# Spreading 23 guard bounds over the rows by a store to DRAM and a broadcast load

## The chip, the cores and the metric

The kernel runs on one core of a Trainium2 chip. The metric is device time in microseconds for one execution, measured over three runs; a profiled execution beside them gives the trace. The engines are called as in the profile: PE (TensorE matmul), PEld (its weight loads), DVE (VectorE), ACT (ScalarE), POOL (GpSimd) and SP (SyncE, which here only issues DMAs).

## The reference

Two attention blocks over 2048 rows with 32 heads of 32, whose outputs stand side by side.

```python
# A: plain multi-head attention
qkv = x @ wqkv                       # x 2048x1024, wqkv 1024x3072
scores = q @ k.T * Dh ** -0.5        # per head, 2048x2048
o = softmax(scores) @ v
a = o @ wo
# B: four segments of 512 rows, causal attention in each, and a memory
for s in range(4):
    p = softmax(qs @ ks.T * scale + mask)
    a_dot = p @ vs
    a_mem = phi(qs) @ M / (phi(qs) @ z + 1e-6)
    o = g * a_mem + (1 - g) * a_dot  # g = sigmoid(beta), per head
    M, z = M + phi(ks).T @ vs, z + sum(phi(ks))
b = o @ wo
return concatenate([a, b], axis=-1)
```

Here phi(t) is t + 1 for positive t and exp(t) otherwise.

## The kernel before, in words

**Units of work.** Part A is worked in groups g of four heads (8 groups) and blocks c of 256 queries (8 blocks); part B in segments s and groups j. For each set of tiles PE makes scores in PSUM (line 964, four heads side by side), ACT turns them into P by an exponential (line 1044, up to 128 x 1024 at a time), and PE multiplies P by V and by ones (the PV rounds of lines 1140 and 1147, in one accumulator bank). P lies in a ring of 20 buffers of 512 columns, so that an exponential writes a buffer only when the PV rounds that read its old content are done. 118 tiles take a cubic instead of an exponential, on DVE and POOL (lines 1002 to 1007).

**The shared bank.** Six PSUM banks hold scores and one the PV accumulators. Bank 6 (X_BANKS) is left for everything else: the projections of K, Q and V, the output projections, the memory's products, and the guard blocks. Each job has a turn: PE fills the bank (line 601 for the projections, through `steps`), DVE empties it (line 1315), and the next job follows. `xbank()` opens a turn.

**The guards.** The softmax subtracts no maximum. In its place each block of keys and queries has a bound, minus half the scale times the sum of the largest squared norms of k and of q, and a flag that tells whether any bound is low enough to matter. Every exponential has two forms, plain and with the bound as its bias. At the first exponential of a block ACT waits for the flag, loads it (line 559) and branches; as long as no flag is set it runs the plain form. A guard block has two steps. `guard_cols` squares and sums K and Q (POOL squares, line 1340 on PE, and a DVE maximum at line 1347), and leaves one column of `cols` with a number for each of 128 rows. `guard_end` has to bring the largest of all rows, or of each half of them, to all rows: DVE copies the column 32 wide into `dg` (line 1384, rounded up by UP because dg is bf16), PE multiplies it by `pick` into a further turn of bank 6 (the spread, line 1393, four matmuls for each column), and DVE takes the maximum out of PSUM (line 1401). Three or four tiny DVE steps make the bias (lines 1407 to 1414) and the flag (line 1418).

There are 27 guard blocks. Four stand in the start of part A and are urgent (`guard_more` and the first quarter). The other 23 are the groups 1 to 7 of part A (`guard_A`, two columns each, one for K and one for Q) and the four pairs of groups in each of the four segments of part B (one column each, K in the first 64 rows and Q in the last 64).

**The order.** No engine's program is written by hand. The code plans operations with keys, durations and dependencies; `level` spreads the jobs between release and due times, and `Prog.schedule` simulates the five engines and writes out one fixed order for each. Its constants (lead times such as LEAD_A, the list NUDGE of due times for single jobs, PHI_AT, AHEAD and others) steer that order. Each engine then runs its order strictly, waiting on semaphores. All DMAs but a few at the start and the end are issued by SP, in one order, so that one that waits holds up those behind it.

Of the kernel before, what the change touches and what calls it, by code (L numbers as in the profile page):

```python
# [6 lines left out]
dt = mybir.dt  # L7
ACT = mybir.ActivationFunctionType
ALU = mybir.AluOpType
AX = mybir.AxisListType  # L10

P = 128
# [24 lines left out]
CARRY = 7  # L37
WHOLE = (("A", 7, 7), ("A", 7, 6))
BCK = 9.626
SOON = 0.124  # L40

PAIR = ((6, 0), (6, 1), (6, 2), (7, 0), (7, 1), (7, 2), (7, 3), (6, 3), (7, 4), (6, 4), (7, 5), (6, 5), (6, 6), (7, 6), (6, 7), (7, 7))
# [113 lines left out]
PV_T = 1.269  # L156
PV_HOT = 1.702
NORM_K = 8.667
JOB_AT = 0.555
# [6 lines left out]
BACKLOG = 2.178  # L166
XR = 9.514
XC = 2.153
STEP = 1.785
OUT3 = 72.703  # L170
OT_STEP = 3
NUDGE = {('KB', 3, 1): 8.43, ('VB', 1, 1): 0.75, ('OB', 0, 0): 7.19, ('OA', 1): 11.77, ('OB', 2, 0): 12, ('KB', 1, 0): 7.83, ('OA', 4): -20.99, ('KA', 5): -6.03, ('KB', 3, 2): 0.67, ('OA', 3): -6.14, ('OA', 5): -5.41, ('VB', 0, 0): -25, ('phi', 3, 1): 4.71, ('KB', 3, 3): 2.86, ('KB', 2, 2): -3.03, ('OA', 0): 0.43, ('VB', 2, 0): 8.32, ('phi', 0, 1): -1.72, ('KB', 1, 1): -7.02, ('phi', 1, 1): 2.49, ('phi', 3, 3): -10.68, ('VB', 1, 0): -3.92, ('OB', 0, 1): 5.6, ('VB', 2, 1): 5.84, ('OB', 3, 0): -0.92, ('VB', 3, 1): -7.84, ('OB', 1, 1): -3.29, ('OB', 1, 0): 1.78, ('KB', 1, 2): -2.71, ('phi', 0, 0): -0.27, ('VB', 0, 1): 9.83, ('OB', 3, 1): 1.59, ('phi', 2, 2): -0.46, ('KB', 2, 1): 8.53, ('VA', 1): -0.13, ('KA', 2): -0.38, ('KB', 2, 0): -4.12, ('phi', 2, 3): 1.64, ('phi', 3, 0): 0.15, ('phi', 0, 2): 3.99, ('phi', 1, 2): -2.16, ('phi', 2, 1): 0.4, ('OA', 2): 6.02, ('phi', 0, 3): -4.43, ('KB', 1, 3): -0.65, ('phi', 1, 0): 0.24, ('KB', 0, 1): -2.16}
SAFE = 0
WOA_STEP = 3
OUT_D = 66.869
M_AT = 4.042
V0_R = 4.52
V0_D = 11.868
FREED = 0.5
VFREED = 11.963  # L180


class Prog:
# [385 lines left out]
class _Kernel:  # L569
# [7 lines left out]
    def sb(self, name, shape, dtype=dt.bfloat16):  # L577
        return self.es.enter_context(self.nc.sbuf_tensor(name, shape, dtype))
# [92 lines left out]
    def alloc(self):  # L671
        nc = self.nc
        sb = self.sb
# [81 lines left out]
        self.bias = sb("bias", [P, 64], dt.float32)  # L755
        self.r_bias = {}
        self.braw = sb("braw", [P, 2], dt.float32)
        self.r_braw = Res()
# [21 lines left out]
        self.sm_last = [self.sem(f"d_last{i}") for i in range(2)]  # L780
        self.sm_PKt = [self.sem(f"d_PKt{i}") for i in range(2)]
        self.sm_OTe = self.sem("d_OTe")

    def plan(self):
        self.plan_constants()
# [203 lines left out]
    def plan_cube(self, t, bank, T):  # L989


        i, j, k = self.ncube % Y_RING, self.ncube % Z_RING, self.ncube % C_RING
        self.ncube += 1
        Y, Z, rY, rZ = self.Y[i], self.Z[j], self.r_Y[i], self.r_Z[j]
        dst, rP = self.Pc[:, k, :], self.r_Pc[k]
        t["P"] = (self.Pc, k, rP)
        bc = t["bias"]
        last = []

        def f(key):  # L1000
# [9 lines left out]
        return (lambda e: e.activation(dst, Y[:, :], ACT.Exp, bias=self.bias[:, 60 + bc:61 + bc], scale=1.0 / KAPPA),  # L1010
                bc, rY, rP, last, t)

    def plan_exp(self, take, slot, buf, T, lo=0, fix=None):
# [364 lines left out]
    def guard_end(self, key, cols, nper, bias_cols, bank=None, urgent=False):  # L1378
        since = len(self.pg.ops)

        dg, rdg = self.dg, self.r_dg
        n = len(cols)
        for i, (c, r) in enumerate(cols):
            self.dve(lambda e, i=i, c=c: e.tensor_scalar(dg[:, i, :], self.cols[:, c:c + 1].to_broadcast([P, 32]), UP, None, ALU.mult),
                     32, key, [r], [rdg], fixed=0.13)
        b = self.xbank() if bank is None else bank

        def spread(e):

            for i in range(n):  # L1390
                for t in range(4):
                    r = slice(32 * t, 32 * t + 32)
                    ins = e.matmul(self.ps[r, 512 * b + 16 * i:512 * b + 16 * i + 16], dg[:, i, :], self.pick[:, :], start=not i, stop=True,
                                   tile_position=(0, 32 * t), skip_group_check=True)
            return ins
# [5 lines left out]
        self.dve(lambda e: e.tensor_reduce(self.cols[:, ci:ci + m],  # L1401
                                           self.ps[:, 512 * b:512 * b + 16 * n].rearrange("p (m r) -> p m r", m=m), AX.X,
                                           ALU.max), 16 * n, key + 0.3, [self.at(b)], [rr])
        for k, bc in enumerate(bias_cols):
            rb = self.r_bias.setdefault(bc, Res())
            raw = self.braw[:, k:k + 1]
            self.dve(lambda e, k=k, raw=raw: e.tensor_scalar(raw, self.cols[:, ci + 2 * k:ci + 2 * k + 1],
                                                             self.cols[:, ci + 2 * k + 1:ci + 2 * k + 2], -0.5 * SCALE,
                                                             ALU.add, ALU.mult), 1, key + 0.4, [rr], [self.r_braw], fixed=0.2)
            self.last_bias = self.dve(lambda e, bc=bc, raw=raw: e.scalar_tensor_tensor(  # L1410
                out=self.bias[:, bc:bc + 1], in0=raw, scalar=-FREE, in1=raw, op0=ALU.is_lt, op1=ALU.mult), 1, key + 0.4,
                [self.r_braw], [rb], fixed=0.3)
            if bc < 2:
                self.dve(lambda e, bc=bc: e.tensor_scalar(self.bias[:, 60 + bc:61 + bc], self.bias[:, bc:bc + 1], ROOT, None, ALU.add), 1,
                         key + 0.4, [rb], [self.r_biasr[bc]])
            nf = self.nflag
            self.nflag += 1
            o = self.dve(lambda e, nf=nf, raw=raw: e.scalar_tensor_tensor(
                out=self.flags[:, nf + 1:nf + 2], in0=raw, scalar=-FREE, in1=self.flags[:, nf:nf + 1], op0=ALU.is_lt, op1=ALU.max), 1,
                key + 0.4, [self.r_braw, self.r_flags], [self.r_flags], fixed=0.17)  # L1420
            self.flag_of[bc] = (nf, o, self.flags[0:1, nf + 1:nf + 2])
        for o in self.pg.ops[since:]:
            if o.eng == "DVE" and urgent:
                o.urgent = True


    def plan_prologue(self):
        self.r_cols = [Res() for _ in range(64)]
# [371 lines left out]
    def plan_jobs(self):  # L1800
# [44 lines left out]
        for s in range(NSEG):  # L1845
# [125 lines left out]
```

## Time and profile before

| What | Value |
|---|---|
| Time, median of three runs | 1117.63 us (1117.24 to 1118.58) |
| Time of the profiled execution | 1116.0 us |
| Span of the profiled execution | 1114.3 us |
| Busy: ACT, PE, DVE, POOL | 1068.6, 1035.5, 732.8, 676.3 us |
| DMA | 72.00 MB, mean 65 GB/s |
| Mean granted clock of TensorE | 0.998 |

The span runs from the first to the last instruction that the profiler recorded. Busy time is the union of an engine's instructions; matmuls overlap in the pipeline, so PE's share is not its distance to a peak. In the groups of instructions a row gives the line, the engine, the operation, what it writes and reads with the shapes, and the count; then the busy time in us and the mean of one in ns, and last the idle time of the engine just before these instructions and what ended it. A line of waits gives who waited for what: us in total, times, and the longest. A line of DMA issues gives the size and the median us from issue to landing. In the window rows each engine has busy time and count, and the granted clock, the DMA share and GB/s stand last.

### The profile page before, as it was taken

How to read it: one execution, taken by the hardware profiler on the slowest of the kernel's cores; microseconds unless marked ns; L12 is line 12 of the kernel's file. 1: busy time of each engine (PE TensorE's matmuls, PEld its weight loads, DVE VectorE, ACT ScalarE, POOL GpSimd, SP SyncE). 2: the span in 40 equal slices, each digit the busy share in tenths (PEclk: the TensorE clock that was granted, in tenths of full speed). 3: DMA queues.
4: the chain of work that ended last, by engine and by line, in shares of the span. 5: the costliest groups of instructions: out<-in, count | busy, mean ns of one | idle time of the engine just before them, and what ended most of it. 6: DMA issues, size and time to landing. Idle time of an engine off the chain costs nothing.

```text
span 1114.3 us, 55312 instructions
## 1 busy us (share of the span) xinstructions
PE 1035.5 (93%) x25332; PEld 558.1 (50%) x25332; DVE 732.8 (66%) x1567; ACT 1068.6 (96%) x1224; POOL 676.3 (61%) x654
## 2 busy tenths in 40 slices
PE   8999999999999988899899988999899899899998
PEld 4456545555545544456455444556455444444554
DVE  3345667766675587877775787777744867856544
ACT  4989999999999999999999999999999899999997
POOL 2224676856576575866666686775845777747421
PEclk9999999999999999999999999999999999999999
DMA  9032351015213230132322320143030351012201
GB/s 208 10 85 49 79 126 24 15 19 122 63 48 88 65 94 12 24 80 57 93 49 63 97 52 18 24 83 88 17 87 29 103 190 41 20 45 62 79 23 54
DMA packets 171098, 72.00 MB, mean 65 GB/s; under 512 B 134768, under 2 KB 169072, under 8 KB 170864
## 3 DMA queue, kind: packets, MB, share of 16 engines
q1 hardware_dynamic: 168496, 67.66, 24.5%
q8 instruction: 199, 3.26, 1.2%
q10 hardware_dynamic: 2368, 0.79, 0.3%
q14 instruction: 35, 0.29, 0.1%
HBM read 45.23 MB, written 11.67 MB: 51 GB/s over the span
## 4 chain that ended last, share of the span: by engine, by line
ACT 44%; PE 40%; DVE 8%; POOL 4%; issue 2%; SPq 1%; DMA 0%; ACTq 0%; DVEq 0%
ACT P L1044 42%; PE ps L601 19%; PE ps L964 8%; PE ps L1140 6%; PE ps L1147 5%; PE ps L1563 1%; POOL Z L1005 1%; DVE Pc L1007 1%; ACT PKQ_B L1607 1%; DVE PKQ_B L1612 1%; SPq L1284 1%; DVE rc L1172 1%; POOL Z L1006 1%; DVE Y L1002 1%; POOL P L1064 1%
## 5 line engine op out<-in xcount | busy, mean ns | idle before, releaser
L1044 ACT ACTIVATE P<-ps 128x1024 bf16<-128x1024 f32 (+1 forms) x1176 | 1041.9, 1084 | 25.7 <-PE ps L1147 19.5
L1147 PE MATMUL ps<-P,onesb 128*32 128x256 bf16 (+1 forms) x4628 | 296.6, 270 | 0.0
L1005 POOL TENSOR_SCALAR Z<-Y 128x512 f32<-128x512 f32 x118 | 181.5, 1538 | 167.2 <-DVE Y L1002 164.5
L1140 PE MATMUL ps<-P,V_A 128*32 128x256 bf16 x3860 | 254.0, 274 | 5.4 <-DVE T L1168 2.3
L964 PE MATMUL ps<-KQ_A 32*128 32x256 bf16 x4096 | 203.4, 273 | 27.8 <-ACT P L1044 20.4
L1006 POOL TENSOR_TENSOR Z<-Z,Y 128x512 f32<-128x512 f32 x118 | 152.4, 1292 | 4.8
L1147 PEld LDWEIGHTS ps<-P,onesb 128*32 128x32 bf16 x4628 | 129.4, 97 | 36.2 <-issue 13.3
L964 PEld LDWEIGHTS ps<-KQ_A 32*128 32x128 bf16 x4096 | 61.4, 92 | 169.9 <-ACT P L1044 139.2
L601 PE MATMUL ps<-xT_B,W_B 128*32 128x512 bf16 (+1 forms) x2232 | 139.3, 366 | 2.1 <-DVE cols L1347 1.2
L601 PE MATMUL ps<-xT_A,W_A 128*32 128x512 bf16 (+1 forms) x2236 | 136.4, 363 | 3.8 <-DVE KQ_A L1315 1.2
L1002 DVE TENSOR_SCALAR Y<-ps 128x512 f32<-128x512 f32 x118 | 81.4, 690 | 79.8 <-PE ps L964 78.5
L1140 PEld LDWEIGHTS ps<-P,V_A 128*32 128x32 bf16 x3860 | 108.6, 96 | 42.5 <-issue 14.2
L1064 POOL TENSOR_SCALAR_AFFINE_SELECT P<-P 128x768 bf16<-128x768 bf16 (+1 forms) x96 | 76.2, 797 | 78.7 <-ACT P L1044 77.6
L1329 POOL TENSOR_TENSOR sqA<-KQ_A 128x512 bf16<-128x512 bf16 x61 | 65.6, 1079 | 93.5 <-DVE KQ_A L1315 64.8
L1007 DVE SCALAR_TENSOR_TENSOR Pc<-Z,Y 128x512 bf16<-128x512 f32 x118 | 105.2, 892 | 21.4 <-POOL Z L1006 14.8
L1329 POOL TENSOR_TENSOR sqB<-KQ_B 128x512 bf16<-128x512 bf16 x64 | 71.1, 1114 | 44.9 <-DVE KQ_B L1315 33.1
L1165 DVE STREAM_TRANSPOSE T<-ps 128x256 f32<-128x256 f32 (+1 forms) x148 | 71.9, 487 | 21.3 <-PE ps L1147 12.9
L601 PEld LDWEIGHTS ps<-xT_A,W_A 128*32 128x32 bf16 x2236 | 52.0, 96 | 53.2 <-issue 15.8
L601 PEld LDWEIGHTS ps<-xT_B,W_B 128*32 128x32 bf16 x2232 | 51.0, 96 | 51.1 <-issue 20.6
L1180 DVE STREAM_TRANSPOSE T<-rc 128x256 f32<-128x256 f32 (+1 forms) x152 | 72.0, 478 | 2.3
L1315 DVE CAST KQ_B<-ps 128x512 bf16<-128x512 f32 x64 | 44.0, 688 | 44.5 <-PE ps L601 44.0
L601 PE MATMUL ps<-Wv_B,xT_B 128*32 128x512 bf16 (+1 forms) x1132 | 68.6, 361 | 1.9 <-DVE KQ_B L1315 1.1
(106 smaller groups left out, 1306.5 us busy)
## 6 DMA issues: line engine op xcount, KB each, us to landing
Wv_B<-in_B_wv_dram SPq DMA_DIRECT2D x32, 256.0 KB, 3.4
W_B<-in_B_wk_dram SPq DMA_DIRECT2D x32, 256.0 KB, 3.0
W_B<-in_B_wq_dram SPq DMA_DIRECT2D x32, 256.0 KB, 3.9
Wo_B<-in_B_wo_dram SPq DMA_DIRECT2D x32, 256.0 KB, 2.9
out_dram<-outsb SPq DMA_DIRECT2D x56, 128.0 KB, 1.8
W_A<-in_A_wqkv_dram SPq DMA_DIRECT2D x14, 256.0 KB, 3.0
ot_a_scratch<-OTst SPq DMA_DIRECT2D x50, 64.0 KB, 2.1
xT_A<-ot_a_scratch SPq DMA_DIRECT2D x6, 512.0 KB, 3.7
```

The source lines that it names most:

```text
L601: ins = e.matmul(out[r], w[:, r], x, start=start, stop=stop, tile_position=(0, 32 * t), skip_group_check=True)
L964: ins = e.matmul(out, kap, qap, start=st, stop=True, tile_position=(32 * h, 0), skip_group_check=True)
L1002: o = self.dve(lambda e: e.tensor_scalar(Y[:, :], src, KAPPA * SCALE, -KAPPA * ROOT, ALU.mult, ALU.add), 512, key - 9.0, [self.bank[bank]] ...
L1005: self.pool(lambda e: e.tensor_scalar(Z[:, :], Y[:, :], CUBE_A, None, ALU.add), 512, key - BCK, [rY], [rZ], rate=0.38)
L1006: self.pool(lambda e: e.tensor_tensor(Z[:, :], Z[:, :], Y[:, :], ALU.mult), 512, key - BCK, [rY, rZ], [rZ], rate=0.435)
L1007: last.append(self.dve(lambda e: e.scalar_tensor_tensor(out=dst, in0=Z[:, :], scalar=CUBE_B, in1=Y[:, :], op0=ALU.add, op1=ALU.mult), 512, ...
L1044: a = self.act(guarded if early else lambda e: e.activation(dst, src, ACT.Exp, scale=SCALE), cols, key, rd, wr, fixed=EXP_FIXED)
L1064: self.pool(lambda e: e.affine_select(v, v, pattern=pat, compare_op=ALU.is_ge, fill=0.0, base=0, channel_multiplier=-1), 2 * nd * P, key + ...
L1140: ins = e.matmul(self.ps[32 * h:32 * h + 32, 512 * obk + q0:512 * obk + q0 + nq], v, p, start=first, stop=last, tile_position=(0, 32 * h), ...
L1147: ins = e.matmul(self.ps[32 * h:32 * h + 32, lcol + q0:lcol + q0 + nq], self.onesb[:, 0:32], p, start=False, stop=last, tile_position=(0, ...
L1180: self.dve(lambda e: e.transpose(T2[:, 0:n].rearrange("p (b r) -> p b r", r=32), bc), n, key, [rr], [r2], fixed=0.17)
L1329: self.pool(lambda e: e.tensor_tensor(sq[:, :], src, src, ALU.mult), 512, key, [rsrc], [rs], rate=0.5)
```

## The change

For the 23 blocks that are not urgent, `guard_end` no longer copies the column, spreads it on PE and reduces it from PSUM. SP stores each column (128 numbers of 4 bytes, one from each partition) to a row of a small DRAM tensor, then loads one or two rows back into the tile `gb` on all 128 partitions, and DVE takes the maxima from there. The step with UP is left out there, since the column is not rounded. The four urgent blocks keep the old way, which moves to a function `spread`. The bias tile shrinks from 64 columns to 24. The planner's constants are set anew: some 20 single numbers, the list NUDGE, and one swap of two neighbours in PAIR, the order of the last sixteen units of part A; it is told 2.5 us of latency for each of the two DMAs.

```diff
-PHI_AT = 6.978
+PHI_AT = 8.238
...
-SOON = 0.124
+SOON = 0.181
...
-PAIR = (..., (6, 4), (7, 5), (6, 5), (6, 6), ...)
+PAIR = (..., (6, 4), (6, 5), (7, 5), (6, 6), ...)
...
-ROW_LEAD = 1.017
-AHEAD = 23.295
-HEAT = 0.681
+ROW_LEAD = 0.722
+AHEAD = 25
+HEAT = 0.867
...
-OVER = 1.64
+OVER = 0.679
...
-RX0 = 34.374
-LEAD_A, LEAD_B, DUE_AT, DUE_SLOPE = 14.219, 8.77, 8.001, 0.1
+RX0 = 25
+LEAD_A, LEAD_B, DUE_AT, DUE_SLOPE = 9.238, 8.77, 10.318, 0.1
...
+GW_LAT, GR_LAT = 2.5, 2.5
...
+        self.gb = sb("gb", [P, 2, P], dt.float32)
+        self.r_gb, self.r_Gd = Res(), [Res(), Res()]
+        self.Gd = nc.dram_tensor("guard_scratch", [2, P], dt.float32)
...
     def guard_end(self, key, cols, nper, bias_cols, bank=None, urgent=False):
-        dg, rdg = self.dg, self.r_dg
         n = len(cols)
-        for i, (c, r) in enumerate(cols):
-            self.dve(lambda e, i=i, c=c: e.tensor_scalar(dg[:, i, :], self.cols[:, c:c + 1].to_broadcast([P, 32]), UP, None, ALU.mult),
-                     32, key, [r], [rdg], fixed=0.13)
-        b = self.xbank() if bank is None else bank
-
-        def spread(e):
...
-        self.last_ge = self.pe(spread, 0.04 * n, key, [rdg, self.r_c], [self.at(b)])
         m = n * nper
         ci = 16 + 8 * (self.nge % 4)
         self.nge += 1
         rr = self.r_cols[ci]
-        self.dve(lambda e: e.tensor_reduce(self.cols[:, ci:ci + m],
...
+        if urgent:
+            self.spread(cols, n, m, ci, rr, key, bank)
+        else:
+            for i, (c, r) in enumerate(cols):
+                self.dma(lambda e, i=i, c=c: e.dma_start(self.Gd[i, :], self.cols[:, c:c + 1]), self.sm_Gw[i], key, [r], [self.r_Gd[i]],
+                         lat=GW_LAT)
+            src = self.Gd[0:n, :]
+            src = bass.AP(tensor=src.tensor, offset=src.offset, ap=[[0, P], [1, P * n]])
+            gb = self.gb[:, 0:n, :].rearrange("p a b -> p (a b)")
+            self.dma(lambda e: e.dma_start(gb, src), self.sm_Gr, key + 0.01, self.r_Gd[0:n], [self.r_gb], lat=GR_LAT)
+            self.dve(lambda e: e.tensor_reduce(self.cols[:, ci:ci + m], gb.rearrange("p (m r) -> p m r", m=m), AX.X, ALU.max), P * n,
+                     key + 0.3, [self.r_gb], [rr])
...
+    def spread(self, cols, n, m, ci, rr, key, bank):
+        dg, rdg = self.dg, self.r_dg
...
```

More of the change, by code (lines that the diff above doesn't have):

```diff
@@ L149 @@
 WIN = 3.413
-ROW_LEAD = 1.017
-AHEAD = 23.295
-HEAT = 0.681
+ROW_LEAD = 0.722
+AHEAD = 25
+HEAT = 0.867
 STICK = 0.616
-OVER = 1.64
+OVER = 0.679
 PV_ROOM = 3.546
-PV_T = 1.269
+PV_T = 1.396
 PV_HOT = 1.702
-NORM_K = 8.667
-JOB_AT = 0.555
+NORM_K = 8.246
+JOB_AT = 0.745
 JOB_SLOPE = 0.617
@@ L162 @@
 RXJ = 4
-RX0 = 34.374
-LEAD_A, LEAD_B, DUE_AT, DUE_SLOPE = 14.219, 8.77, 8.001, 0.1
+RX0 = 25
+LEAD_A, LEAD_B, DUE_AT, DUE_SLOPE = 9.238, 8.77, 10.318, 0.1
 HOLD = {}
-BACKLOG = 2.178
+BACKLOG = 2.534
 XR = 9.514
[L168 to L172, printed above, removed]
@@ new lines @@
+XC = 1.667
+STEP = 2.002
+OUT3 = 68.392
+OT_STEP = 1.384
+NUDGE = {('KB', 3, 1): 8.43, ('VB', 1, 1): 0.75, ('OB', 0, 0): 7.19, ('OB', 2, 0): 12, ('KB', 1, 0): 7.83, ('OA', 4): -22.26, ('KA', 5): -6.03, ('OA', 3): -6.14, ('OA', 5): -5.41, ('VB', 0, 0): -18.85, ('phi', 3, 1): -1.02, ('KB', 3, 3): 2.86, ('KB', 2, 2): -4.83, ('OA', 0): 0.43, ('VB', 2, 0): 8.32, ('phi', 0, 1): -1.72, ('KB', 1, 1): -4.4, ('phi', 1, 1): 2.49, ('VB', 1, 0): -13.99, ('OB', 0, 1): 5.6, ('OB', 3, 0): -0.92, ('VB', 3, 1): -7.84, ('OB', 1, 1): -2.15, ('OB', 1, 0): 1.78, ('KB', 1, 2): -2.71, ('VB', 0, 1): 6.76, ('OB', 3, 1): 1.59, ('phi', 2, 2): -0.46, ('KB', 2, 1): 8.53, ('VA', 1): -2.65, ('KA', 2): -0.38, ('KB', 2, 0): 3.59, ('phi', 2, 3): 0.58, ('phi', 3, 0): -0.27, ('phi', 0, 2): 3.99, ('phi', 1, 2): -2.16, ('phi', 2, 1): 5.04, ('OA', 2): 6.02, ('phi', 0, 3): -4.43, ('KB', 1, 3): -3.5, ('phi', 1, 0): 3.2, ('KB', 0, 1): -2.16, ('KB', 0, 3): -2.11, ('KB', 0, 2): 3.63, ('phi', 1, 3): 4.85, ('VA', 3): 4.64, ('KB', 0, 0): -8.08, ('KB', 2, 3): -4.95, ('phi', 3, 2): 0.59, ('KA', 6): -0.42}
@@ L173 @@
 SAFE = 0
 WOA_STEP = 3
-OUT_D = 66.869
+OUT_D = 63.577
 M_AT = 4.042
-V0_R = 4.52
+GW_LAT, GR_LAT = 2.5, 2.5
+V0_R = 4.492
 V0_D = 11.868
 FREED = 0.5
-VFREED = 11.963
+VFREED = 9.044
 class Prog:
@@ L754, in alloc @@
         self.r_dg = Res()
-        self.bias = sb("bias", [P, 64], dt.float32)
+        self.bias = sb("bias", [P, 24], dt.float32)
+        self.gb = sb("gb", [P, 2, P], dt.float32)
+        self.r_gb, self.r_Gd = Res(), [Res(), Res()]
+        self.Gd = nc.dram_tensor("guard_scratch", [2, P], dt.float32)
         self.r_bias = {}
@@ L782, in alloc @@
         self.sm_OTe = self.sem("d_OTe")
+        self.sm_Gw = [self.sem(f"d_Gw{i}") for i in range(2)]
+        self.sm_Gr = self.sem("d_Gr")
     def plan(self):
@@ L1009, in plan_cube @@
         self.item(T + 0.001, f)
-        return (lambda e: e.activation(dst, Y[:, :], ACT.Exp, bias=self.bias[:, 60 + bc:61 + bc], scale=1.0 / KAPPA),
+        return (lambda e: e.activation(dst, Y[:, :], ACT.Exp, bias=self.bias[:, 20 + bc:21 + bc], scale=1.0 / KAPPA),
                 bc, rY, rP, last, t)
@@ L1379, in guard_end @@
         since = len(self.pg.ops)
-        dg, rdg = self.dg, self.r_dg
         n = len(cols)
-        for i, (c, r) in enumerate(cols):
-            self.dve(lambda e, i=i, c=c: e.tensor_scalar(dg[:, i, :], self.cols[:, c:c + 1].to_broadcast([P, 32]), UP, None, ALU.mult),
-                     32, key, [r], [rdg], fixed=0.13)
-        b = self.xbank() if bank is None else bank
-        def spread(e):
[L1390 to L1395, printed above, removed]
-        self.last_ge = self.pe(spread, 0.04 * n, key, [rdg, self.r_c], [self.at(b)])
         m = n * nper
@@ L1413, in guard_end @@
             if bc < 2:
-                self.dve(lambda e, bc=bc: e.tensor_scalar(self.bias[:, 60 + bc:61 + bc], self.bias[:, bc:bc + 1], ROOT, None, ALU.add), 1,
+                self.dve(lambda e, bc=bc: e.tensor_scalar(self.bias[:, 20 + bc:21 + bc], self.bias[:, bc:bc + 1], ROOT, None, ALU.add), 1,
                          key + 0.4, [rb], [self.r_biasr[bc]])
@@ L1424, in guard_end, with mm @@
                 o.urgent = True
+    def spread(self, cols, n, m, ci, rr, key, bank):
+        dg, rdg = self.dg, self.r_dg
+        for i, (c, r) in enumerate(cols):
+            self.dve(lambda e, i=i, c=c: e.tensor_scalar(dg[:, i, :], self.cols[:, c:c + 1].to_broadcast([P, 32]), UP, None, ALU.mult),
+                     32, key, [r], [rdg], fixed=0.13)
+        b = self.xbank() if bank is None else bank
+        def mm(e):
+            for i in range(n):
+                for t in range(4):
+                    r = slice(32 * t, 32 * t + 32)
+                    ins = e.matmul(self.ps[r, 512 * b + 16 * i:512 * b + 16 * i + 16], dg[:, i, :], self.pick[:, :], start=not i, stop=True,
+                                   tile_position=(0, 32 * t), skip_group_check=True)
+            return ins
+        self.last_ge = self.pe(mm, 0.04 * n, key, [rdg, self.r_c], [self.at(b)])
+        self.dve(lambda e: e.tensor_reduce(self.cols[:, ci:ci + m],
+                                           self.ps[:, 512 * b:512 * b + 16 * n].rearrange("p (m r) -> p m r", m=m), AX.X,
+                                           ALU.max), 16 * n, key + 0.3, [self.at(b)], [rr])
     def plan_prologue(self):
```

4 lines of the change are left out of this document (1 added, 3 removed).

## The prediction

> **What bounds the kernel now.** I read the page first: the busy shares, then the chain of work that ended last.
>
> ```profile
> span 1114.3 us, 55312 instructions
> ...
> PE 1035.5 (93%) x25332; PEld 558.1 (50%) x25332; DVE 732.8 (66%) x1567; ACT 1068.6 (96%) x1224; POOL 676.3 (61%) x654
> ...
> ACT 44%; PE 40%; DVE 8%; POOL 4%; issue 2%; SPq 1%; DMA 0%; ACTq 0%; DVEq 0%
> ```
>
> ScalarE (ACT) is the engine that sets the time: it works 1068.6 of 1114.3 us, and the change takes no exponential away and adds none. So all that can be won or lost is ACT's idle time, 1114.3 - 1068.6 = 45.7 us. The chain says who causes it: it runs through ACT for 44% of the span and through TensorE (PE) for 40%, so the two take turns as the bound. Next I asked what ACT waited for.
>
> ```profile
> ACT P L1044 <- PE ps L1147: 19.5, 22, 3.7
> ...
> ACT P L1044 <- PE ps L964: 4.8, 8, 1.7
> ```
>
> In the steady part ACT waits 19.5 + 4.8 = 24.3 us, in 30 pieces; the other 21.4 us of idle time are the start and the end, where the urgent guard blocks keep their bank turn. The larger number needs reading. L964 makes the scores that an exponential reads, but L1147 sums the rows of P that an earlier exponential wrote. An exponential that waits for L1147 waits for a buffer of the ring of 20 in P to come free: PE is so far behind with its PV rounds that ACT has filled the ring. So 19.5 of the 24.3 us are PE backlog, and what PE no longer has to do comes off them, as far as such a wait follows. Nothing in this view waits for a guard bound or for a DMA.
>
> One wait is of another kind. Three windows around it, with the busy time of PE, PEld, DVE, ACT, POOL, and the granted clock after that:
>
> ```profile
> 882.40:885.90 3.50, 1.84 (x44) 0.67 (x32) 3.13 (x8) 3.12 (x4) 3.50 (x4) 0.99 0.26 59
> 885.90:889.30 3.40, 3.36 (x40) 1.54 (x44) 3.40 (x6) 1.02 (x1) 3.40 (x4) 0.50 0.32 99
> 889.30:892.70 3.40, 3.40 (x108) 2.17 (x104) 2.74 (x9) 2.09 (x3) 3.40 (x5) 1.00 0.51 135
> ```
>
> PE was busy 1.84 of 3.5 us, and in the next 3.4 us the granted clock was 0.50; ACT lost 0.38 + 2.38 + 1.31 = 4.1 us over the three. That is this trace's price for one badly packed stretch.
>
> **The change, part by part.** 23 guard blocks change: 7 for part A with two columns each (groups 1 to 7) and 16 for part B with one, so 30 of the 34 columns. Their groups:
>
> ```profile
> L1384 DVE TENSOR_SCALAR dg<-cols 128x32 bf16<-128x32 f32 x34 | 13.9, 407 | 0.6
> L1347 DVE TENSOR_REDUCE cols<-ps 128x1 f32<-128x512 f32 x18 | 12.3, 686 | 7.2 <-PE ps L1340 5.9 <-PE ps L1140 0.7 <-PE ps L1147 0.6
> L1347 DVE TENSOR_REDUCE cols<-ps 128x1 f32<-128x128 f32 x16 | 4.6, 285 | 3.6 <-PE ps L1340 3.5
> L1401 DVE TENSOR_REDUCE cols<-ps 128x2 f32<-128x16 f32 x20 | 3.4, 169 | 4.4 <-PE ps L1393 4.4
> L1401 DVE TENSOR_REDUCE cols<-ps 128x2 f32<-128x32 f32 x7 | 1.2, 175 | 0.6 <-PE ps L1140 0.5
> L1393 PE MATMUL ps<-pick,dg 128*32 128x16 bf16 x136 | 5.3, 177 | 3.0 <-DVE KQ_B L1315 1.5 <-DVE OT_B L1633 1.0 <-DVE KQ_A L1315 0.3
> ```
>
> *PE, removed.* 30 x 4 = 120 of the 136 matmuls of L1393 go: 5.3 x 120/136 = 4.7 us. After a spread, PE also waits until its reduce has emptied the bank:
>
> ```profile
> PE ps L601 <- DVE cols L1401: 1.6, 4, 0.8
> ...
> PE ps L601 <- DMA xT_A<-in_A_x_dram: 1.1, 2, 0.7
> ...
> PE ps L964 <- DVE cols L1401: 1.1, 2, 0.6
> ```
>
> That is 2.7 us for 27 blocks, so 2.7 x 23/27 = 2.3 us. The 3.0 us ahead of the spreads (the idle column of L1393) I count as nothing: they are waits for the previous tenant's eviction, and the projection that now follows needs the same bank, so the wait passes on to it. At best 3.0 x 23/27 = 2.6 us go too. PE thus saves 4.7 + 2.3 = 7.0 us, between 4.7 and 9.6. How much of that reaches ACT? PE carries 40% of the chain, so I take 0.40 x 7.0 = 2.8 us; the ends are nothing and all 9.6 us, well inside the 24.3 us that ACT waits.
>
> *DVE, removed and added.* 30 copies to dg go (30 x 0.407 = 12.2 us) and 23 small reduces (3.4 + 1.2 less four of 0.17 = 3.9 us). In their place come 16 reduces over 128 elements, priced by the 128x128 reduce (0.285 us each, 4.6 us), and 7 over 256, between 0.285 and the 0.686 us of 512, so about 0.49 us each (3.4 us). Both rows read PSUM and the new ones read SBUF, an uncertainty of a tenth of a microsecond each at most. DVE saves 12.2 + 3.9 - 8.0 = 8.1 us; with 8% of the chain that is 0.6 us.
>
> *DMA, added.* 30 stores of 0.5 KB and 23 broadcast loads (64 or 128 KB into SBUF), all on SP. Nothing like the store, 128 pieces of 4 bytes, is in the trace; its nearest rows are the 64 KB store and, for the load, the broadcast of beta. The last row is the spread of the weight loads of L1269, which SP often has in flight at that moment:
>
> ```profile
> ot_a_scratch<-OTst SPq DMA_DIRECT2D x50, 64.0 KB, 2.1
> ...
> graw<-in_B_beta_dram SPq DMA_DIRECT2D x1, 8.0 KB, 2.5
> ```
>
> ```profile
> DMA to landing us min/median/max: 2.7/3.5/5.3
> ```
>
> I take 2.1 + 2.5 = 4.6 us for the pair on a quiet queue, 3.5 + 3.5 = 7.0 us behind bulk loads, and 10.6 us as the far end. On SP the store waits for its column and the load waits for the store, and all that stands behind them in SP's order waits too: weight loads, OT stores, output stores. SP already stands for long at the head of its line:
>
> ```profile
> SPq L1236 <- POOL OTst L1231: 222.1, 38, 23.8
> SPq L1687 <- DVE outsb L1315: 198.8, 51, 30.5
> ```
>
> And the only wait of PE for a DMA in the whole program is the 1.1 us at the start, quoted above. So a delay of 2 us on SP is covered by loads that land early, and I cost it at nothing; without that cover each of 23 blocks could hold a load up by the 2.1 us of a store.
>
> *The way from column to bound.* This is what the change trades. A block of part B in the trace of before, on DVE:
>
> ```profile
> 398.31 0.28 DVE L1347 TENSOR_REDUCE cols<-ps 128x1 f32<-128x128 f32 x1
> ...
> 398.67 0.56 DVE L1384 TENSOR_SCALAR dg<-cols 128x32 bf16<-128x32 f32 x1
> ...
> 401.26 0.69 DVE L1315 CAST KQ_B<-ps 128x512 bf16<-128x512 f32 x1 [0.33 <-PE ps L601]
> ...
> 403.85 0.17 DVE L1401 TENSOR_REDUCE cols<-ps 128x2 f32<-128x16 f32 x1
> ...
> 404.23 0.20 DVE L1407 TENSOR_SCALAR braw<-cols 128x1 f32<-128x1 f32 x1
> ...
> 404.46 0.65 DVE L1410 SCALAR_TENSOR_TENSOR bias<-braw 128x1 f32<-128x1 f32 x1
> 405.03 0.15 DVE L1418 SCALAR_TENSOR_TENSOR flags<-braw,flags 128x1 int32<-128x1 f32 x1
> ```
>
> From the column (398.59) to the flag (405.18) 6.6 us pass, most of them because another projection (evicted at 401.26) takes the bank in between. The new way has no bank in it: 4.6 us of DMA, 0.29 for the reduce, and 0.20 + 0.65 + 0.15 = 1.0 for the rest, 5.9 us; behind bulk loads 7.0 + 1.3 = 8.3 us, at the far end 11.9 us. So on a quiet queue the bound is no later than now. What a late one costs shows where ACT needs a bound at once:
>
> ```profile
> 901.45 0.29 DVE L1347 TENSOR_REDUCE cols<-ps 128x1 f32<-128x128 f32 x1
> ...
> 907.61 0.15 DVE L1418 SCALAR_TENSOR_TENSOR flags<-braw,flags 128x1 int32<-128x1 f32 x1
> ```
>
> ```profile
> L559 ACTq TENSOR_LOAD <-flags x1: 280/280/280, 907.8 to 907.8; - x1
> ```
>
> ```profile
> 892.56 0.15 DVE L1418 SCALAR_TENSOR_TENSOR flags<-braw,flags 128x1 int32<-128x1 f32 x1
> ```
>
> ```profile
> L559 ACTq TENSOR_LOAD <-flags x1: 283/283/283, 892.7 to 892.7; - x1
> ```
>
> Column at 901.74, flag at 907.76, and ACT loads it at 907.8: 6.0 us, with no slack on its queue. Group 7's flag, written at 892.71, is loaded at 892.7 as well. A way of 5.9 us just holds this, one of 8.3 us is 2.3 us late. The traffic moves this price: the Trainium skill, in "DMA: Bandwidth & Descriptors", section "Latency and other measured facts", gives 0.2 us for an HBM access on average and 2 us at high load; by it, an estimate, a store beside bulk loads would be 1.8 us slower than the quiet one and such a block 1.7 us late. No run here shows it yet.
>
> *The retuned constants and the swapped pair.* They change the order that the planner writes out, and no row prices that. ACT's work is the same. I set it at nothing, with 4.1 us to either side: the stretch at 882 to 893 us may go, or one like it may come.
>
> *Sum.* 2.8 + 0.6 = 3.4 us less. The profiled execution took 1116.0 us (span and 1.7 us around it), so 1112.6; the median of the three runs lies 1.6 us above it, so **1114.2 us**. The own range of this case is from a gain of 9.6 us to one of 2.2: 1108.0 to 1115.4.
>
> **Rivals.** *Late bounds.* A segment's first block comes late and PE, with no scores to make room for, falls under half load as at 882 us, so that its clock is halved. Two places have no slack (892 and 908 us): 2 x 2.3 = 4.6, and 4.1 for one stretch at half clock, less the 3.4: 5.3 us slower, 1122.9. It decides from where store and load together take over 6.0 - 1.3 = 4.7 us. For it: the rows give 4.6, at the very edge, weight loads follow each guard block, and both places lie where the last window above shows 135 GB/s, over a mean of 65 in the table above. Against it: the planner carries 2.5 us for each of the two DMAs, and can move the block ahead.
> Of the clock the Trainium skill ("TensorE: Matmul & The Clock Gate", Part 1) says that it is halved after at least one idle window of about 3.4 us. The trace differs: PE was busy 1.84 of 3.5 us and was halved all the same. By that rule a lateness of 2.3 us costs no clock, so that this case ends at 4.6 - 3.4 = 1.2 us slower, 1118.8, within what I call no change; I give that 0.03.
>
> *Nothing to see.* PE's saved time goes into waits for the same bank (the 3.0 us pass on, and the 2.3 us come back behind the column's own reduce), 0.4 x 4.7 = 1.9 us are left: 1115.7, under what can be told.
>
> *The bank is the bound.* Then each turn counts in full. PE at the block above:
>
> ```profile
> 403.61 0.19 PE L1393 MATMUL ps<-pick,dg 128*32 128x16 bf16 x4 [0.97 <-DVE OT_B L1633]
> ...
> 404.17 0.40 PE L601 MATMUL ps<-xT_B,W_B 128*32 128x512 bf16 x4
> ```
>
> From spread to the next projection 0.56 us; 23 x 0.56 = 12.9 us: 1104.7. For it: nearly all of L601's work goes through one bank. Against: PE fills a bank's pauses with PV rounds.
>
> **How the numbers follow.** Forecast 0.50, late bounds 0.27, nothing to see 0.13 (with the 0.03), the bank as the bound 0.10. About 0.2%, 2.2 us, is what a measurement of this kernel can tell from no change. Faster is 0.50 + 0.10 = 0.60, no change 0.13, slower 0.27. The range goes from 1107.0, the end of the forecast's own range with a microsecond of allowance towards the bank's case, to 1122.0, which leaves out the bank's case and a third of the late one.
>
> **What would show it.** Right: L1393 with 16 matmuls; ACT's waits for L1147 and L964 near 21 us; stores landing in about 2.1 us and loads in 2.5; no gap of ACT at a flag. Wrong: pairs of DMAs over 4.7 us with ACT gaps or a second window at clock 0.50 at a segment's start; or steady waits that stay at 24 us with fewer PE instructions; or an order that puts new gaps where no guard block is near.

## The result and the profile after

The changed kernel takes 1300.44 us in the median of six runs (1294.38 to 1302.52), against 1117.68 us before: a ratio of 1.163, 95% interval 1.160 to 1.166. The forecast of 1114.2 us was wrong in sign, and the time lies far outside its range. The profiled execution took 1294.4 us. Where a ratio further down does not match the medians, it is made of the fast runs alone.

The page of the changed kernel, its span, busy shares, and the chain that ended last:

```profile
span 1292.7 us, 55369 instructions
...
PE 1096.3 (85%) x25324; PEld 576.8 (45%) x25324; DVE 723.5 (56%) x1537; ACT 1075.9 (83%) x1224; POOL 677.9 (52%) x654
...
PE 38%; ACT 24%; DMA 22%; DVE 9%; issue 4%; POOL 1%; another core or an unknown queue 1%; SPq 1%; ACTq 0%; DVEq 0%
ACT P L1050 22%; PE ps L602 20%; DMA guard_scratch<-cols 13%; DMA gb<-guard_scratch 9%; PE ps L970 7%; PE ps L1146 5%; PE ps L1153 5%; DVE Y L1008 1%; SPq L1290 1%; ACT PKQ_B L1628 1%; DVE T L1171 1%; DVE Pc L1013 1%; PE ps L1584 1%; DVE cols L1353 1%
```

ACT, DVE and POOL work about as long as before; they wait more. ACT is idle for 1292.7 - 1075.9 = 216.8 us where it was 45.7. PE alone is busy longer, by 60.8 us, although it has 120 matmuls fewer to do: its mean granted clock fell from 0.998 to 0.938. DMA had 0% of the chain and has 22%, all of it the two guard transfers. What ACT and DVE waited for:

```profile
ACT P L1050 <- PE ps L970: 128.4, 60, 8.6
ACT P L1050 <- remote: 23.5, 8, 4.6
ACT P L1050 <- PE ps L1153: 22.6, 18, 3.7
...
ACT P L1050 <- DVE bias L1415: 7.9, 1, 7.9
```

```profile
DVE cols L1403 <- DMA gb<-guard_scratch: 131.1, 23, 8.5
```

The waits for a free P buffer (L1153) hardly moved. What grew is the wait for scores (L970), from 4.8 to 128.4 us: PE no longer delivers in time. "Remote" marks waits whose releaser the profile can't name; ACT had none of them before. Each of these ended with a step of the counter that PE alone raises, so they are waits for PE too. And DVE has a wait that did not exist: it stands 131.1 us, in each of the 23 blocks, at the reduce that reads `gb`. One block shows how the two belong together. SP, DVE, PE and ACT, in this order, in the timeline of the changed kernel:

```profile
167.88 0.52 SPq L1397 DMA_DIRECT2D guard_scratch<-cols  x1
...
176.20 1.43 SPq L1402 DMA_DIRECT2D gb<-guard_scratch  x1
```

```profile
173.55 0.69 DVE L1321 CAST KQ_B<-ps 128x512 bf16<-128x512 f32 x1 [0.93 <-PE ps L602]
182.10 0.29 DVE L1403 TENSOR_REDUCE cols<-gb 128x2 f32<-128x128 f32 x1 [7.87 <-DMA gb<-guard_scratch]
182.31 0.44 DVE L1171 STREAM_TRANSPOSE T<-ps 128x256 f32<-128x256 f32 x1
```

```profile
183.23 0.40 PE L1146 MATMUL ps<-P,V_B 128*32 128x256 bf16 x4 [6.00 <-DVE T L1174]
```

```profile
185.51 1.94 ACT L1050 ACTIVATE P<-ps 128x1024 bf16<-128x1024 f32 x2 [6.82 <-PE ps L970]
```

The store is issued at 167.88 and the load only at 176.20, when the store has landed: 8.3 us. DVE has come to the reduce at 174.2 and stands until 182.1. Behind the reduce, in DVE's fixed order, is the copy that empties the accumulator bank; PE needs that bank, stands 6.0 us, and has the next scores behind it; ACT loses 6.8 us. What ACT waited for were scores, not the bound.

PE's pause has a second price. Two windows of the same stretch, with the busy time of PE, PEld, DVE, ACT and POOL, and the granted clock after that:

```profile
177.20:180.40 3.20, 0.03 (x4) 0.00 (x0) 0.00 (x0) 1.49 (x2) 0.56 (x1) 1.00 0.60 142
180.40:187.20 6.80, 3.97 (x64) 2.00 (x68) 4.26 (x15) 1.69 (x2) 2.12 (x3) 0.50 0.55 130
```

PE works at a granted clock of 0.50 for 6.8 us behind its pause. The trace of the changed kernel has 28 such stretches, 160.4 us in all, where the one of before has a single one of 3.4 us.

The store is slow with next to nothing else under way. In the stretch that begins with these two lines of SP, the packets that began from 939 to 945.2 us are counted below them:

```profile
937.77 0.34 SPq L1397 DMA_DIRECT2D guard_scratch<-cols  x1
945.32 0.34 SPq L1402 DMA_DIRECT2D gb<-guard_scratch  x1
```

```profile
DMA packets 0, 0.00 MB, mean 0 GB/s; under 512 B 0, under 2 KB 0, under 8 KB 0
```

Its packets are gone after a microsecond and none begins for six more, but it has not landed until 7.5 us after its issue. One packet of instructions, begun just before at 938.95, was under way until 942.2; its 3.2 us are twice the longest of before, 1.6. From a store to the issue of its load that is the shortest of the 23; the longest is 12.1 us. The load's landing in the changed kernel, shortest, median, longest:

```profile
DMA to landing us min/median/max: 2.9/4.8/6.5
```

### The profile page after: what moved, and what is told of

Read it like the earlier page. It is cut to its first block, busy times and chain, and to the rows that moved or that the text cites. A ratio compares the mean times of both kernels' runs of the same rounds, so it can differ in the third digit from the quotient of the medians.

```text
span 1292.7 us, 55369 instructions
## 1 busy us (share of the span) xinstructions
PE 1096.3 (85%) x25324; PEld 576.8 (45%) x25324; DVE 723.5 (56%) x1537; ACT 1075.9 (83%) x1224; POOL 677.9 (52%) x654
## 4 chain that ended last, share of the span: by engine, by line
PE 38%; ACT 24%; DMA 22%; DVE 9%; issue 4%; POOL 1%; another core or an unknown queue 1%; SPq 1%; ACTq 0%; DVEq 0%
ACT P L1050 22%; PE ps L602 20%; DMA guard_scratch<-cols 13%; DMA gb<-guard_scratch 9%; PE ps L970 7%; PE ps L1146 5%; PE ps L1153 5%; DVE Y L1008 1%; SPq L1290 1%; ACT PKQ_B L1628 1%; DVE T L1171 1%; DVE Pc L1013 1%; PE ps L1584 1%; DVE cols L1353 1%
## 5 line engine op out<-in xcount | busy, mean ns | idle before, releaser
L1050 ACT ACTIVATE P<-ps 128x1024 bf16<-128x1024 f32 (+1 forms) x1176 | 1046.4, 1053 | 196.5 <-PE ps L970 128.4
L1153 PE MATMUL ps<-P,onesb 128*32 128x256 bf16 (+1 forms) x4628 | 312.0, 278 | 5.3 <-issue 5.2
L1146 PE MATMUL ps<-P,V_A 128*32 128x256 bf16 x3860 | 264.8, 280 | 11.1 <-DVE T L1174 4.1
L970 PE MATMUL ps<-KQ_A 32*128 32x256 bf16 x4096 | 210.4, 280 | 36.0 <-ACT P L1050 13.5
L602 PE MATMUL ps<-xT_B,W_B 128*32 128x512 bf16 (+1 forms) x2280 | 148.9, 378 | 29.7 <-DVE KQ_B L1321 9.6
L1153 PEld LDWEIGHTS ps<-P,onesb 128*32 128x32 bf16 x4628 | 133.7, 99 | 41.4 <-issue 19.3
L602 PE MATMUL ps<-xT_A,W_A 128*32 128x512 bf16 (+1 forms) x2248 | 142.3, 372 | 11.0 <-DVE KQ_A L1321 6.3
L970 PEld LDWEIGHTS ps<-KQ_A 32*128 32x128 bf16 x4096 | 62.2, 93 | 189.7 <-ACT P L1050 130.0
L1171 DVE STREAM_TRANSPOSE T<-ps 128x256 f32<-128x256 f32 (+1 forms) x148 | 71.9, 486 | 36.4 <-PE ps L1153 15.5
L602 PE MATMUL ps<-Wv_B,xT_B 128*32 128x512 bf16 (+1 forms) x1124 | 74.8, 382 | 13.3 <-DVE V_B L1321 6.9
L602 PE MATMUL ps<-Wo_B,OT_B 128*32 128x512 bf16 (+1 forms) x1156 | 74.5, 372 | 9.2 <-DVE outsb L1321 8.4
L1403 DVE TENSOR_REDUCE cols<-gb 128x2 f32<-128x128 f32 (+1 forms) x23 | 7.5, 327 | 131.1 <-DMA gb<-guard_scratch 131.1
```

The costliest lines, as they stand in the source:

```text
L602: ins = e.matmul(out[r], w[:, r], x, start=start, stop=stop, tile_position=(0, 32 * t), skip_group_check=True)
L970: ins = e.matmul(out, kap, qap, start=st, stop=True, tile_position=(32 * h, 0), skip_group_check=True)
L1050: a = self.act(guarded if early else lambda e: e.activation(dst, src, ACT.Exp, scale=SCALE), cols, key, rd, wr, fixed=EXP_FIXED)
L1146: ins = e.matmul(self.ps[32 * h:32 * h + 32, 512 * obk + q0:512 * obk + q0 + nq], v, p, start=first, stop=last, tile_position=(0, 32 * h), ...
L1153: ins = e.matmul(self.ps[32 * h:32 * h + 32, lcol + q0:lcol + q0 + nq], self.onesb[:, 0:32], p, start=False, stop=last, tile_position=(0, ...
L1171: self.dve(lambda e: e.transpose(T2[:, 0:n], src), n, nk, rsrc, [r2], fixed=0.17)
```

## The experiments

Four theories were put to the test. A: DVE's fixed order holds the reduce too early. B: the retuned constants make a poor order. C: the small transfers hold up SP and the others; once C was seen to hold a part, it was split into D (the stores of 4-byte pieces keep the DRAM busy), E (SP stands at each load until the store has landed) and F (the broadcast load). All ratios are to the kernel before, on the same chip, with 95% intervals.

### Tell the planner the true durations (true_lat)

```diff
-GW_LAT, GR_LAT = 2.5, 2.5
+GW_LAT, GR_LAT = 8.0, 5.0
```

> The changed kernel, but the planner is told 8.0 us for the store and 5.0 us for the load in place of 2.5 and 2.5, as the trace of the changed kernel shows them; nothing else differs. Theory A (DVE's fixed order holds the reduce about 7 us before its data are there, and all that DVE does for PE waits behind it): DVE's idle time ahead of the reduce falls from 131.1 us to under 30, and the time to 1120 to 1160 us, with a rest at places where ACT needs a bound early. Theory B (the retuned constants make a poor order) and theory C (the small DMAs hold up SP and the other transfers): 1280 us or more, as with the change.

Measured: 1222.77 us, ratio 1.094 (1.092 to 1.096). DVE's wait at the reduce, 131.1 us before, is now

```profile
DVE cols L1403 <- DMA gb<-guard_scratch: 11.7, 3, 7.6
```

So A is right about the wait, and taking it away came with a gain of 78 us. Not all of that need be DVE's: the order is another one, and SP's standing at the loads fell as well, from 111.4 to 37.9 us. And the time stays 60 us over what A alone allows. A is not the whole cause.

### The constants alone (retune_bank)

```diff
-        if urgent:
+        if True:
             self.spread(cols, n, m, ci, rr, key, bank)
```

> The changed kernel's constants, but all 27 guard blocks take the old way through bank 6 on PE; no guard DMA. Theory A and theory C: within 1% of the kernel before, 1107 to 1129 us. Theory B: 1280 us or more.

Measured: 1125.28 us, ratio 1.007 (1.006 to 1.009). B falls as the main cause. The constants cost 8 us with the old way, and ACT's waits show it in small pieces: L1153 23.9 us for 19.5, L970 8.2 for 4.8.

```profile
ACT P L1050 <- PE ps L1153: 23.9, 24, 3.7
...
ACT P L1050 <- PE ps L970: 8.2, 13, 1.3
```

### The new way with the old constants (path_alone)

All 21 lines of constants are those of the kernel before; the new `guard_end` and its two latencies stay.

> The kernel before with its own constants, and only the new way through DRAM for the 23 blocks (2.5 and 2.5 us told to the planner). Theory A: DVE waits about 23 x 5.7 us = 130 us ahead of the reduce again, and the time is 1240 to 1310 us. Theory B: within 1% of before, 1107 to 1129 us. Theory C: about 1290 us, but with little idle time of DVE ahead of the reduce.

Measured: 1319.98 us, ratio 1.182 (1.180 to 1.183). B is out; the new way does it alone, and is 20 us dearer without the retuning. DVE waits 151.9 us at the reduce, 23 times; A's wait is there, though the time lies 10 us above A's range.

### Transfers that nobody reads (dma_unread)

```diff
-        if urgent:
-            self.spread(cols, n, m, ci, rr, key, bank)
-        else:
+        self.spread(cols, n, m, ci, rr, key, bank)
+        if not urgent:
...
-            self.dve(lambda e: e.tensor_reduce(self.cols[:, ci:ci + m], gb.rearrange("p (m r) -> p m r", m=m), AX.X, ALU.max), P * n,
-                     key + 0.3, [self.r_gb], [rr])
```

> The changed kernel with its 30 stores and 23 loads, but nobody reads what they bring: the bounds go through bank 6 as before. What is left of the change is its traffic and its place in SP's queue. Theory A: 1110 to 1140 us. Theory C: 1250 us or more. Theory B: 1280 us or more.

Measured: 1226.96 us, ratio 1.099 (1.097 to 1.102). No instruction of an engine depends on these transfers, and yet they cost 110 us, some 100 more than the constants. A does not allow that; C does, short of its 1250. ACT's "remote" waits are here too, 36.4 us of them, and PE's counter ended each one. PE's waits of a kind that the kernel before knew once, for 0.7 us, are here

```profile
PE ps L1153 <- issue: 19.2, 8, 4.1
PE ps L602 <- issue: 16.8, 11, 3.4
PE ps L1146 <- issue: 7.9, 6, 2.7
```

"Issue" is time in which PE waited for nothing that the profile shows. One of them, in the order of time on SP and on PE, comes while a store is on its way:

```profile
91.60 0.34 SPq L1396 DMA_DIRECT2D guard_scratch<-cols  x1
...
93.91 0.58 SPq L1275 DMA_DIRECT2D W_B<-in_B_wq_dram  x1
100.41 0.34 SPq L1401 DMA_DIRECT2D gb<-guard_scratch  x1
```

```profile
96.25 0.28 PE L1146 MATMUL ps<-P,V_A 128*32 128x256 bf16 x4
100.58 0.35 PE L1153 MATMUL ps<-P,onesb 128*32 128x256 bf16 x4 [4.06 <-issue]
```

PE stops at 96.5 and goes on at 100.6, just after the store has landed (the load behind it is issued at 100.41). A load of weights issued in that stretch landed after 9.6 us; the median before was 3.0.

```profile
W_B<-in_B_wk_dram SPq DMA_DIRECT2D x1, 256.0 KB, 9.6
```

The program's own instructions come by DMA too. Their 199 packets of 16 KB took 1.2% of the 16 engines' span before (1.1 us each) and here 1.4% of a longer one (1.4 us each). Before, the longest took 1.6 us; here 25 of them take over 2 us, and 24 of the 25 are under way within 10 us of a store's issue. Of PE's "issue" waits here, 20 are over 0.8 us; 17 of them fall within 10 us of a store's issue, but only in 9 is an instruction packet under way. So the stores are behind most of these waits; that late instructions are what links the two fits about half of them and is not shown.

```profile
q8 instruction: 199, 3.26, 1.4%
```

### The stores alone (store_only), and with their pieces apart (store_apart)

The first is the run before without the 23 loads. The second also changes where the 128 numbers go:

```diff
-        self.Gd = nc.dram_tensor("guard_scratch", [2, P], dt.float32)
+        self.Gd = nc.dram_tensor("guard_scratch", [2, P, P], dt.float32)
...
-                self.dma(lambda e, i=i, c=c: e.dma_start(self.Gd[i, :], self.cols[:, c:c + 1]), ...
+                self.dma(lambda e, i=i, c=c: e.dma_start(self.Gd[i, :, 0:1], self.cols[:, c:c + 1], ...
```

> The kernel of the unread DMAs (bounds through bank 6, the changed kernel's constants) without its 23 loads: the 30 stores of 128 pieces of 4 bytes are issued and nobody waits for them. Theory D (such a store keeps the DRAM busy for about 8 us and delays what other transfers read meanwhile, weights and instructions): 1190 to 1235 us, with PE and ACT gaps of 2 to 5 us after stores. Theory E (SP stands at each load until its store has landed, and what is queued behind comes late): 1120 to 1135 us, since SP no longer waits. Theory F (the broadcast load from one row is the burden): 1120 to 1135 us.

> As the run with the stores alone, but the 128 pieces of 4 bytes go to places 512 bytes apart instead of side by side in one row of 512 bytes. If the pieces are slow because they share a row: about 1125 us, as with the constants alone. If each piece of 4 bytes is slow wherever it lands: 1190 to 1235 us.

Measured: the stores alone 1210.25 us, ratio 1.076 (1.069 to 1.083); with the pieces 512 bytes apart 1125.53 us, ratio 1.009 (1.006 to 1.011), which is what the constants cost by themselves. So the stores carry it, not E and F: 30 stores that nobody waits for cost 6.9% (1.076 less 1.007), some 77 us, over the constants, and the same 30 with the same bytes cost nothing once their pieces do not lie side by side. The size is less sure than the cause: the four times of the stores alone lie between 1194 and 1214 us. What they do to others shows in the loads of weights. With the stores alone, such a load issued within 7 us behind a store landed after 9.9 us (median of the 23 whose landing the profile gives), any other after 3.2; in the run with the unread pairs it is 10.0 and 3.2, and with the pieces apart 3.7 and 3.2. That it is the DRAM that is kept busy, as D has it, no run shows. PE's wait for "issue" is back to one, and no "remote" wait is left:

```profile
PE ps L602 <- issue: 0.6, 1, 0.6
```

### The loads alone (load_only)

```diff
...
-            src = self.Gd[0:n, :]
-            src = bass.AP(tensor=src.tensor, offset=src.offset, ap=[[0, P], [1, P * n]])
...
+            src = self.A_x[0]
+            src = bass.AP(tensor=src.tensor, offset=src.offset, ap=[[0, P], [1, 2 * P * n]])
...
```

The 30 stores are left out.

> The kernel of the unread DMAs without its 30 stores: the 23 broadcast loads read 512 or 1024 bytes of the input x instead, 128 times each, and nobody waits for them. Theory D and theory E: 1120 to 1135 us. Theory F: 1190 us or more, with landings over 4 us.

Measured: 1125.12 us, ratio 1.008 (1.007 to 1.010). F falls: 128 partitions that read one row cost nothing here, and such a load lands in 2.8 to 4.7 us, 3.0 in the median.

### How far apart, and what SP's standing costs (apart_wait, apart64_wait)

Both add to store_apart the loads of load_only, each waiting on SP for its store; the second puts the pieces 64 bytes apart.

> The stores with their pieces 512 bytes apart, and now each with a load that waits for it on SP (it reads x, and nobody reads what it brings; the bounds go through bank 6). This shows how long such a store takes to land and what SP's standing at the load is worth. Theory D: the load is issued 2 to 3 us after its store, and the time stays within 0.5% of the run without the loads (1125.5). Theory E: over 1140 us.

> The same with the pieces 64 bytes apart, so that 8 of them share 512 bytes. If pieces hinder each other only within 64 bytes: load issued 2 to 3 us after the store, time near 1125 us. If within 512 bytes: a landing of about 3 us and over, up to the 7.5 us of the change, and a time between 1125 and 1225 us.

Measured: 1125.94 us, ratio 1.008 (1.005 to 1.010), and 1126.32 us, ratio 1.009 (1.008 to 1.011). The store lands after 1.4 to 3.6 us at 512 bytes and 1.4 to 4.0 us at 64; side by side the load followed it after 7.5 to 12.1. SP's waits for the stores at the line of the load add up to 18.5 us in the run with 64 bytes, where the changed kernel has 111.4:

```profile
SPq L1401 <- DMA guard_scratch<-cols: 18.5, 11, 3.3
```

So a distance of 64 bytes is enough to set the pieces apart; in the change 16 of them lay in each 64 bytes. Distances between 4 and 64 bytes were not tried, so where the slowness begins is open. The Trainium skill ("DMA: Bandwidth & Descriptors", section "Specifications") says that transfers under 512 bytes are read, modified and written back. That alone does not make the store slow: pieces of 4 bytes at a distance of 64, eight in each 512 bytes, land after 2.3 us in the median, about as fast as any store here. SP's standing with such a short landing costs nothing; what it costs with the slow one was not tried by itself. The 2.3% between the stores alone (1.076) and the unread pairs (1.099) are the loads and this standing together; the spread of the stores alone makes that 1 to 3%.

### The same way with whole rows stored (row_store)

```diff
...
+                gw, gt = self.gb[:, i, 0:32], self.gb[:, i, 32:64]
+                self.dve(lambda e, gw=gw, c=c: e.tensor_copy(gw, self.cols[:, c:c + 1].to_broadcast([P, 32])), 32, ...
+                self.dve(lambda e, gw=gw, gt=gt: e.transpose(gt, gw), 32, ...
-                self.dma(lambda e, i=i, c=c: e.dma_start(self.Gd[i, :], self.cols[:, c:c + 1]), ...
+                self.dma(lambda e, i=i: e.dma_start(self.Gd[i, :].rearrange("(a b) -> a b", b=32), self.gb[0:P:32, i, 32:64]), ...
```

> The changed kernel with one step altered: DVE copies the column 32 wide and transposes it in blocks of 32, so that the store writes 4 pieces of 128 bytes from 4 partitions instead of 128 pieces of 4 bytes; load, reduce, constants and the 2.5 us told to the planner stay. Theory D: the store lands in 2 to 3 us, DVE's wait ahead of the reduce falls from 131 us to under 40, and the time to 1120 to 1150 us. Theory E gives a part of that, as SP's wait at the load shortens with the landing. Theory F: the landing of the load stays at 4.4 us and over, DVE waits 50 us or more and the time stays over 1200 us.

Measured: 1132.82 us, ratio 1.015 (1.013 to 1.017). The same 512 bytes go to the same place in 4 pieces of 128, and of the 183 us 168 are gone. The load now follows its store after as little as 1.5 us, and DVE's wait at the reduce is

```profile
  DMA gb<-guard_scratch: 9.0, 8
```

DVE's wait thus followed from the slow store: with a store and a load near what the planner had been told, DVE's order fits.

### The repaired way with the old constants (row_store_old, row_store_old_lat)

The store by rows with the constants of the kernel before, once with 2.5 and 2.5 us told, once with 3.0 and 3.2.

> The store by rows (4 pieces of 128 bytes) with the constants of the kernel before, told 2.5 and 2.5 us. Theory D and the bookkeeping so far (constants 0.7%, the rest of the new way 0.7%): 1118 to 1132 us. If the bank turn was worth what the forecast took for it: 1112 to 1117 us.

> The same, with the planner told what the run by rows shows: 3.0 us for the store, 3.2 us for the load. DVE's wait ahead of the reduce falls under its 9.0 us with 2.5 and 2.5; time 1112 to 1128 us, and below the run with 2.5 and 2.5 if that wait matters.

Measured: 1127.79 us, ratio 1.009 (1.008 to 1.011), and 1136.53 us, ratio 1.017 (1.015 to 1.019). Neither beats the bank turn. The second lies over the 1128 us that it was given, and tells more: half a microsecond more for one latency and 0.7 for the other, nearer to the truth, and the planner's order comes out 9 us worse, while DVE's wait at the reduce fell only from 7.6 to 6.8 us.

### No spread at all (no_spread, no_spread_old)

```diff
+            for i, (c, r) in enumerate(cols):
+                self.dve(lambda e, i=i, c=c: e.tensor_copy(self.cols[:, ci + i * nper:ci + (i + 1) * nper],
+                                                           self.cols[:, c:c + 1].to_broadcast([P, nper])), 16, key + 0.3, [r], [rr])
```

This stands in place of store, load and reduce.

> Leaves part of the computation out: the 23 bounds are not spread over the rows at all, neither through the bank nor through DRAM; one tiny DVE copy stands in place of the reduce, and each row keeps its own number. The changed kernel's constants. If the forecast's gain side holds (3.4 us from PE, bank and DVE): 1118 to 1123 us, that is 2 to 7 us under the run with the same constants and the bank turn (1125.3). If the order that the planner writes decides and the freed time is worth nothing: 1123 to 1132 us.

> The same with the constants of the kernel before. Gain side: 1109 to 1114.5 us, 2 to 8 us under the kernel before. Order decides: 1115 to 1128 us, at or over the kernel before although 120 matmuls and 23 bank turns are gone.

Measured: 1137.64 us, ratio 1.019 (1.018 to 1.021), with the new constants, and 1128.00 us, ratio 1.010 (1.008 to 1.012), with the old ones. The first lies even above the range for a freed time that is worth nothing, the second in that range. A kernel that has lost 120 matmuls, 23 bank turns and 23 reduces is 1% slower. ACT's waits for a P buffer went up, not down, in the second:

```profile
ACT P L1050 <- PE ps L1153: 25.1, 17, 3.8
```

17 waits take 25.1 us, where 22 took 19.5: fewer and longer. That is 5.6 of the 12.6 us by which the span grew; the rest lies in a few single waits of ACT, for scores, for DVE and for POOL. The order is another one, and what it loses outweighs what PE saves. These two runs also answer the rival that the bank is the bound: with 23 turns gone, nothing was gained.

## Why the prediction was wrong

*The bound.* Right: ACT's work stayed (1068.6 us before, 1075.9 after), and the loss is ACT's idle time, 216.8 - 45.7 = 171.1 us of the 178.4 by which the span grew; the rest is a few us more in which its exponentials count as busy.

*PE, removed.* The step was carried out: the spread's matmuls are 16 in the changed kernel, and its reduces from PSUM four. The 3.4 us of gain that the sum made of it do not exist in this program. Taking the spreads away without any DMA gave +1.0% and, against the same constants with the bank turn, 1.9% for 0.7%. The step that failed is "How much of that reaches ACT? PE carries 40% of the chain": that share holds for one order, and a removal makes the planner write another.

*The retuned constants.* Set at nothing with 4.1 us to either side. Measured at +8 us with the bank turn, while they are worth 20 us to the new way itself (1319.98 without, 1300.44 with). An order that is written anew moved the time by 9 to 12 us in three other cases (the two told latencies, the two runs with no spread). The term was mis-sized by two to five times.

*DMA, added.* This is where the sum broke. The store was priced at 2.1 us by a store of 64 KB and, behind bulk loads, at 3.5, with 5.3 as the far end. It took 7.5 to 12.1 us, and 7.5 with no load beside it. The text said that nothing like 128 pieces of 4 bytes is in the trace, and then took the row with the nearest name; what counted was neither the sum of bytes nor the piece's size alone but that the pieces lie side by side: 64 bytes apart the same pieces land in 2.3 us. The sentence of the Trainium skill on HBM at high load ("DMA: Bandwidth & Descriptors", section "Latency and other measured facts"), which the prediction weighed with 1.8 us more, does not cover what happened: the store was slow with no load beside it, and by over 5 us. The load, taken at 2.5 us, lands in 3.0 to 3.3 in the runs without slow stores and in 4.8 behind them (medians).

*"I cost it at nothing."* The cover named was that loads land early. It holds for SP's standing with a short landing (apart_wait). What was left out is that a transfer can slow the others: 30 stores that nobody waits for cost 77 us.

*The wait that the change adds.* The text asked what is queued behind the store and the load on SP, and did not ask it of the reduce on DVE. There it is the bank's eviction and the copy that frees PE's accumulators, and the price is the difference between the changed kernel and the same transfers unread: 1.163 less 1.099 of the time before, about 71 us; by true_lat, which changed more than that wait, it is 78.

*The rivals.* "Late bounds" had the sign and the deciding quantity, store and load over 4.7 us, and the wrong place: it looked for ACT waiting at a flag in two places. ACT waited on DVE's bias once, 7.9 us; 128.4 us were waits for scores, where the same transfers unread have 49.4, and DVE was held in all 23 blocks. The rival also had the half clock, for one stretch at 4.1 us; there were 28, and PE had been busy for at most 0.55 of the 3.4 us before each. (The stretch at 882 us, which the rival calls under half load, was 1.84 of 3.5 us, a little over half.) What these stretches are worth by themselves was not tried apart; they are contained in the figures below.

The account by runs, in per cent of the time before: constants 0.7; stores side by side, unread, 6.9 more; loads and SP's standing behind them 2.3; DVE held at the reduce 6.4; together 16.3. Each of these steps also contains a newly written order, which by itself moved other runs by about 1%.

## What to carry to other kernels

Before a value goes through DRAM, count the pieces in which it is written and where they fall: 512 bytes in 128 neighbouring pieces landed after 7 us at the least and slowed other transfers, in 4 pieces the load could follow after 1.5 to 4.1. A wait put into an engine's fixed order costs what stands behind it on that engine, so look there first, even if the waiting result itself is needed only tens of microseconds later. And where a planner writes the order, a saving of a few us of work could not be forecast from the old order's chain: here every edit without the slow store left the time about 1 to 2% longer, the removal of work included.

## What the runs showed that was not expected

Pieces of 4 bytes side by side in DRAM land slowly: 7.5 us for 128 of them is about 59 ns each, an estimate from that row, as if they were written one after another. At 64 bytes apart the same pieces land in 1.4 to 4.0 us. With the stores alone, loads of weights beside them take 9.9 us in the median for 3.2. With the unread pairs PE stands up to 4.1 us at a time, 44 us in all, for nothing that the profile shows. In the changed kernel its granted clock was 0.50 for 3.4 to 10.2 us, 28 times, each behind 3.4 us in which it was busy for 0.55 of the time or less.
